# Attention followed by a token-mixing MLP: a mask built later, two scalings and one cast on other engines, token mixing three matmuls on

## The chip, the cores and the metric

The kernel runs on one core of a Trainium2 chip. The metric is the device time in microseconds (us) of one launch. Five engines work side by side: TensorE (PE in the profile), VectorE (DVE), ScalarE (ACT), GpSimd (POOL) and SyncE (SP), which here only issues DMAs. GpSimd and ScalarE issue DMAs too. Each engine takes its instructions in the order of its own list, and waits on semaphores for the others.

## The reference

There are 8 batches of 576 tokens, 8 heads of 64. First comes attention with a band of 32 positions to either side and 8 global tokens, which see all and are seen by all; then a residual MLP with a mixing over tokens and one over channels.

```python
scores = scale * np.matmul(q, k.transpose(0, 1, 3, 2))
mask = (np.abs(pos[:, None] - pos[None, :]) <= 32) | is_global[:, None] | is_global[None, :]
attn = softmax(np.where(mask, scores, -1e9))
x = (attn @ v) with the heads side by side            # (8, 576, 512)
tok = np.einsum('ts,bsd->btd', w_tok, alpha1 * x + beta1)
u = x + lam * tok
ch = np.maximum((alpha2 * u + beta2) @ w_ch1, 0.0) @ w_ch2
out = u + lam * ch
```

Inputs and output are fp32; the matmuls are fed in bf16 and fp16.

## The kernel before

**Stages.** The tokens of all batches make 36 tiles of 128 tokens. The channel MLP takes them in 9 groups of 4 tiles (GROUPS, L34): group 0 is batch 0 without its last 64 tokens, group 1 is batch 1 likewise, and a tile ("S", p) holds the last 64 tokens of two batches. A group is 128 steps, called slots here, each with one matmul of 512 columns: slots 0 to 63 compute W1 times the transposed tiles UT into HT (L559 to L567), slots 64 to 127 HT times W2 (L569). While group g runs, the attention and the token mixing of batch g + 1 are woven between its matmuls: `weave` (L84) spreads a list of small functions over a stretch of slots, and `timed` (L1070) does so for loads, transposes and copies. So the order on every engine follows from the slot numbers; there is no other planner. Within one slot the woven functions come before what `timed` put there, and these before the matmul.

**The opening.** Batch 0 has nothing to hide behind. Its order is written by hand: FIRST (L45) is a list of short names, looked up in `ops` (L922) and run from left to right; a name with ":n" uses PSUM bank n, and "sp:n" issues n spare matmuls whose result nobody reads. The names that matter here:
- `ck0..3`, `cq0..3`: casts of K and Q of two heads at a time to bf16 (L618, L622). CK names the engine of each K cast: A is ScalarE, D VectorE, P GpSimd.
- `tk`, `tq`: transposes on TensorE (L633); `kt`, `qv`: their copies out of PSUM (L637, L649).
- `gx` (L257) masks the gathered rows of the global tokens; `gt` (L693) transposes them into bank 1; `ge0` copies global K (L703) and half of global Q (L708) out of it, `ge1` the other half of global Q (L708), `gte` both once more for later (L697).
- `ct` casts the last 64 tokens of K and Q (L927), `tt` transposes them.
- `GM` (L852) builds the mask of the global keys, three instructions on VectorE: a comparison of positions with the global positions into a scratch tile, then two halves of the mask. `G` (L272) multiplies it with the exponentials `eg0`, `eg1` of the global scores in EG.
- `s20` and the like are scores (L351), `e...` their exponentials (L360), `pg`, `pt` masked probabilities (L317, L326), `q` and `pvx`, `pvy` the products with V.
- `va`, `vb` copy V to Vo, shifted by 64 rows.

**Batch 1.** Its attention is woven over slots 12 to 88 of group 0 (`first_attention`, L1038), the row sums of w_tok and the copies of wt4o at slot 89 (`late_rows`, L1031), its token mixing over slots 98 to 112. Each head pair ends with `norm_x`, `norm_y` on VectorE (L427) and `scale_x`, `scale_y`, which multiply by alpha1 * lam into XL (L445, L462, L463). `xl_eng` (L429) chooses the engine of the last two. A token tile (L509) is five matmuls, then `finish_u`:

```python
        nc.vector.tensor_tensor(out=x, in0=ps, in1=x, op=ALU.add)
        ...
        nc.gpsimd.tensor_tensor(out=ub, in0=x, in1=A2, op=ALU.mult)
        nc.sync.dma_start_transpose(out=UT[g % 2][:, :, js], in_=ub)
```

The first matmul of group 1 reads all four transposed tiles in UT.

**Batch 2 in group 0.** Its K, Q and V are loaded by GpSimd from slot 1 on, its K and Q are transposed by DMA from SyncE's queue over slots 44 to 75 (`xbars`, L1060), V is copied to Vo by two DMAs from SyncE's queue (`copy_vo`, L223), the gathered global rows are transposed at slots 98 and 100 (L266), and `qpad` (L234) copies QT to QP on VectorE at slots 101, 105, 109 and 113.

Of the kernel before, what the change touches and what calls it, by code (L numbers as in the profile page):

```python
# [10 lines left out]
FP16 = mybir.dt.float16  # L11
# [3 lines left out]
ALU = mybir.AluOpType  # L15

P = 128
S = 576
# [24 lines left out]
    [(7, 1), (7, 2), ("S", 3), (7, 3)],  # L43
]
FIRST = """  # L45
kgz vez io ktz pgz gb1 gbm:0 W0 gbc ar0 pz1 ar1 gath ck0 ar2 pgc tk0:1 sp:3 cq0 mask idn tq0:2 sp:16 V0 pz3 GM
qv0 V1 pz2 cq1 V2 tq1:3 kt0 cq2 V3 tq2:4 sp:1 ck2 qv1 qv2 ck1 tk2:5 V4 kt2 ck3 tk1:6 wki cq3 gat1 kt1 tk3:0 wi
kt3 gx tq3:2 ct qv3 gt:1 tt:3 sp:3 ge0 gte fz ktt ge1 qtt z20:4 s20:5 gk1:6 e201 la e200 z21:0 z11:2 s11:1
gk0:3 b1t eg1 va1 s21:5 e111 z00:4 s00:6 eg0 z10:1 sp:2 va2 e210 s10:3 vb1 G e211 z01:0 sp:2 e001 s01:5 e100
lb:6 e011 pz0 e010 pg2 z31:1 s31:5 lc v1f qz0 qz1 u0 pt2 ab:0 abe sp:2 e310 q2:6 e000 wt1:1 ra2 wt3:4 sp:2 we1  # L50
pg0 rd2 pvx2:6 e101 vb2 pt0 e311 pvy2:1 e110 q0:3 nx2 we3 wt0:5 pg1 ra0 wt2:2 nr2 ny2 we0 wt4:6 xl2 rd0 we2
q1:4 pt1 z30:1 s30:5 pvx0:3 we4 xm2 pvy0:2 nx0 ra1 rs:6 e300 beta rd1 e301 nr0 pg3 pvy1:1 re pvx1:3 ny0 pt3
xl0 q3:4 tm2:5 ra3 nr1 ny1 kc0 kc1 rd3 xm0 u1 nx1 pvy3:6 pvx3:2 ad2 xl1 tm0:4 nx3 xm1 u2 u3 u4 nr3 ad0 ny3 qc0
qc1 tx2:3 tm1:5 xl3 xm3 tx0:4 ad1 bm0 tm3:6 ut0 ut2 tx1:5 ad3 ut1 bm1 bm2 tx3:4 gc1 ut3 kc2 kc3 b1i qc2 qc3
bm3 W1s bme
"""
PLACE = {t: (g, j) for g, ts in enumerate(GROUPS) for j, t in enumerate(ts)}

# [41 lines left out]
def kernel(ctx, tc, q, k, v, global_idx, alpha1, beta1, w_tok, alpha2, beta2, w_ch1, w_ch2, lam, out):  # L100
    nc = tc.nc
# [8 lines left out]
    def T(name, shape, dt):  # L110
        return cp.tile(list(shape), dt, name=name)
# [19 lines left out]
    C16 = T("C16", [P, S], FP16)  # L131
    C32 = T("C32", c32n.shape, FP32)
# [17 lines left out]
    EG = T("EG", [P, S], FP16)  # L150
    G = T("G", [P, 2, 704], FP16)
    GM = T("GM", [P, 2, S], FP16)
# [8 lines left out]
    HTt = T("HT", [P, 16 * DM], BF16)  # L161
# [5 lines left out]
    mask = T("mask", [P, NW, 64], FP16)  # L167
# [16 lines left out]
    gbc = T("gbc", [P, 8], FP32)  # L184
    gsel = T("gsel", [P, 8], FP32)
    gval = T("gval", [P, 1], FP32)
# [17 lines left out]
    QST = XR[:, 8:12, :].rearrange("p a b -> p (a b)").rearrange("p (h j d) -> p h j d", h=H, j=4)  # L204
    TST = SR[:, 1, :]
    WTB = HTt[0:96, 0 : 6 * S].rearrange("p (c s) -> p c s", c=6)

    def xs(t):
        return SR[:, t[1] % 2, :] if t[0] == "S" else XR[:, 4 * (t[0] % 3) + t[1], :]
# [13 lines left out]
    def copy_vo(b):  # L223
        ve, vo = Ve[b % 2], Vo[b % 2]
        nc.sync.dma_start(out=vo[0:64], in_=ve[64:128, 0:4])
        nc.sync.dma_start(out=vo[64:128], in_=ve[0:64, 1:5])
# [141 lines left out]
    def sc_unit(b, hp, u):  # L368
        def f():
            ps = sc_ps()  # L370
            sc_mm(ps, b, hp, u)
            sc_exp(ps, b, hp, u)
            if u == 2:
                probs_q(b, hp)
                probs_k(b, hp)

        return (0.6, f)
# [14 lines left out]
    def gq_pv(b, hp):  # L392
        def f():
            ps = pv_ps()
            gq_mm(ps, b, hp)
            gq_hi(ps, hp)
            gq_lo(ps, hp)

        return (0.9, f)
# [27 lines left out]
        nc.vector.tensor_tensor(out=xo, in0=pv[:, :, :, 0:64], in1=rb, op=ALU.mult)  # L427

    def xl_eng(b, hp):  # L429
        return nc.vector if (b, hp) in ((0, 3),) else nc.gpsimd  # L430

    def pv_tiles(ps, b, hp, i0, i1):
        for i in range(i0, i1):
# [49 lines left out]
    def pv_y(b, hp):  # L483
        st = {}

        def f3():
            st["ps"] = pv_ps()
            pv_mms(b, hp, 3, st["ps"][:, 0:130])

        def f4():  # L490
            pv_mms(b, hp, 4, st["ps"][:, 130:260])
            norm_y(st["ps"], b, hp)
            scale_y(b, hp)

        return [(0.75, f3), (0.4, f4)]
# [13 lines left out]
    def tok_tile(b, i):  # L509
        par = b % 2  # L510

        def f():
            ps = pv_ps()
            cs = slice(128 * i, 128 * i + 128)
            for s in range(4):
                mm(ps, wtT[:, s, cs], XL[par][:, s, :], s == 0, False)
            mm(ps, wtT[:, 4, cs] if par == 0 else wt4o[:, cs], XL4[par], False, True)
            finish_u((b, i), ps)

        return (1.1, f)  # L520

    def tok_shared(p):
        def f():
            ps = pv_ps()
            for s in range(5):
                for par in range(2):
                    l = wt4o[:, 512:S] if s == 4 and par == 1 else wtT[:, s, 512:S]
                    mm(ps[64 * par : 64 * par + 64, :], l, XL4[par] if s == 4 else XL[par][:, s, :], s == 0, s == 4)
            finish_u(("S", p), ps)

        return [(1.1, f)]

    def gap(w):
        return (w, lambda: None)
# [11 lines left out]
    def token_mix(b):  # L546
        a = [tok_tile(b, i) for i in range(4)]
        if b % 2 == 1:
            a += tok_shared(b // 2)
        return a  # L550
# [103 lines left out]
    def tr_pair(b, hp):  # L654
        def f():
            psq, psk = pv_ps(), pv_ps()
            pair_tr(psq, QB0[b], hp)
            pair_tr(psk, KB0, hp)
            pair_k(psk, b, hp)
            for a in range(2):  # L660
                pair_q(psq, hp, a)

        return (0.6, f)
# [111 lines left out]
    def ld_wt():  # L775
        g_.dma_start(out=WTB, in_=w_tok.rearrange("(j p) s -> p j s", j=6))

# [72 lines left out]
        nc.vector.tensor_tensor(out=mask, in0=bd, in1=m9, op=ALU.mult)  # L850

    def gm():  # L852
        nc.vector.tensor_scalar(out=EG, in0=C16, scalar1=gval[:, 0:1], scalar2=None, op0=ALU.is_equal)
        for a in range(2):
            nc.vector.tensor_scalar(  # L855
                out=GM[:, a, :], in0=EG, scalar1=C32[:, 32 + a : 33 + a], scalar2=C32[:, 34 + a : 35 + a], op0=ALU.mult, op1=ALU.max
            )

    def b0_beta(par, eng):
# [3 lines left out]
    def wtok_tr(ps, k):  # L863
        ps = ps.bitcast(BF16)
        n = 128 if k < 4 else 64
        for j in range(6):
            nc.tensor.transpose(out=ps[0:n, 96 * j : 96 * j + 96], in_=WTB[:, j, 128 * k : 128 * k + n], identity=identb[0:96, 0:96])

# [49 lines left out]
    mlp0 = mlp(0)  # L918
    hb = {}
    CPY = {"A": nc.scalar.copy, "D": nc.vector.tensor_copy, "P": nc.gpsimd.tensor_copy}  # L920
    CK, QV, KC, QC, NY, PZ = "AAAD", "ADDD", "AAAA", "AAPP", "AADA", "PAAA"
    ops = {  # L922
        "idn": lambda: nc.scalar.copy(out=ident, in_=identb),
        "kgz": kz_fill,
# [97 lines left out]
    for w in FIRST.split():  # L1022
        n, _, b = w.partition(":")
# [14 lines left out]
    def first_attention(b):  # L1038
        s = [[sc_unit(b, hp, u) for u in range(3)] for hp in range(HP)]
        t_ = [tr_pair(b, hp) for hp in range(HP)]  # L1040
        q_ = [gq_pv(b, hp) for hp in range(HP)]
        w = [pv_x(b, hp) + pv_y(b, hp) for hp in range(HP)]
        a = [t_[0], tr_tail(b), gap(1.2), t_[1], gap(0.8), s[0][0], t_[2], gap(0.3), s[0][1], s[0][2], t_[3], gap(0.3)]
        a += [s[1][0], s[1][1], s[1][2], gap(0.4)]
        a += [gk_all(b, pv_ps), gap(0.5), q_[0], gap(0.6), s[2][0], s[2][1]] + w[0] + [q_[1], s[2][2], s[3][0], s[3][1]] + w[1] + [q_[2], s[3][2], gap(0.9)]
        return a + w[2][0:3] + [q_[3]] + w[2][3:] + [gap(0.9)] + w[3]
# [30 lines left out]
    for g in range(9):  # L1077
        base = mlp(g) if g else mlp0
        slots = [[] for _ in range(129)]
        nb = g + 2  # L1080
        if nb < NB:
            if g == 0:
                timed(prefetch(nb) + prefetch_v(nb), slots, 1, 42)
            else:
                timed(prefetch(nb), slots, 1, 34)
            timed(xbars(nb), slots, 44, 75)
            slots[78 if g else 118].append(lambda: copy_vo(nb))
            if nb % 2 == 0:
                pr = nb // 2
                slots[1].insert(0, lambda pr=pr: gather(pr))  # L1090
                slots[44] += [lambda: gather_x(0), lambda: gather_x(1)]
                slots[84 if g else 98].append(lambda pr=pr: gather_tr(pr, 0))
                slots[87 if g else 100].append(lambda pr=pr: gather_tr(pr, 1))
            timed([lambda hp=hp: qpad(hp) for hp in range(HP)] + [lambda: gcols(nb)], slots, 89 if g else 101, 105 if g else 122)
            if nb + 1 < NB:
                timed(prefetch_v(nb + 1), slots, 85 if g else 122, 96 if g else 127)

        def wrap(i):
            def f():
                for s in slots[i]:  # L1100
                    s()
                base[i]()

            return f

        items = [wrap(i) for i in range(128)] + base[128:]
        if g == 0:
            for i in range(9):
                items[i] = lambda i=i: [s() for s in slots[i]]
        if g == 0:  # L1110
            parts = [(first_attention(1), 12, 88), ([(1.0, late_rows)], 89, 90), (token_mix(1), 98, 112)]
        elif g + 1 < NB:
            parts = [(attention(g + 1), 2, 83), (token_mix(g + 1), 97, 115 if g < 3 else 122)]
        else:
            parts = []
        weave(items, parts)
# [30 lines left out]
```

## Time and profile before

| | |
|---|---|
| median of 14 runs | 389.71 us |
| lowest and highest | 387.49 and 390.97 us |
| the profiled execution, its own time | 388.54 us |
| its span in the profile | 386.8 us |
| TensorE busy | 375.2 us |
| VectorE, GpSimd, ScalarE busy | 225.3, 210.4, 175.1 us |
| granted clock of TensorE, mean | 0.995 |
| moved by DMA | 47.87 MB, 124 GB/s |

A line of a timeline reads: start (us from the span's start), length, engine, line of the kernel, operation, output<-inputs, shape, how many in a row; in brackets the idle time of the engine just before, and what released it. "SPq" is SyncE issuing a DMA: the time is that of the issue, and the data move later. A line of the list of waits reads: who waited, for whom, total us, how often, longest. Where a mark of landing is named in the text, it is the time at which the trace shows the last of a DMA's completion signals.

### The profile page before, as it was taken

The page shows a single profiled execution, that of the slowest core. Times are in us where ns is not written, and L with a number is a line of the kernel's source. Part 1 is how long each engine was busy: PE and PEld are TensorE (multiplying, and loading weights), DVE is VectorE, ACT ScalarE, POOL GpSimd, SP SyncE. Part 2 cuts the span into 40 slices and gives each one's busy share as a digit, 9 for nine tenths or more (in the row PEclk, how much of TensorE's full clock was granted, in tenths as well). Part 3 has the DMA queues.
Part 4 walks back from the last instruction along what each step waited for, and adds up shares of the span by engine and source line. Part 5 has one row for each costly group of instructions (what it writes and reads, how often), then busy time and mean ns, then how long its engine had stood idle before and what let it go on. Part 6 is the DMA issues. An engine that isn't in the chain of part 4 may idle for free.

```text
span 386.8 us, 8196 instructions
## 1 busy us (share of the span) xinstructions
PE 375.2 (97%) x3120; PEld 208.7 (54%) x3120; DVE 225.3 (58%) x585; ACT 175.1 (45%) x349; POOL 210.4 (54%) x273
## 2 busy tenths in 40 slices
PE   6899999999999999999999999999999999999996
PEld 3469566445654665456545664466456654444443
DVE  7887566984477557945595559545864554014023
ACT  6687874017800881067305840386028700730720
POOL 7978729786668844894388647963241335000000
PEclk9899999999999999999999999999999999999999
DMA  7999999969989994999497999799240013101002
GB/s 238 168 224 271 190 206 143 176 98 183 153 149 147 156 152 95 119 152 151 108 127 127 155 141 101 130 150 146 84 91 20 3 56 81 42 19 63 29 27 81
DMA packets 160836, 47.87 MB, mean 124 GB/s; under 512 B 147537, under 2 KB 154521, under 8 KB 160798
## 3 DMA queue, kind: packets, MB, share of 16 engines
q0 software_dynamic: 98288, 17.05, 66.0%
q1 hardware_dynamic: 61678, 29.71, 37.9%
q10 hardware_dynamic: 832, 0.60, 0.5%
q8 instruction: 24, 0.39, 0.4%
q14 instruction: 14, 0.11, 0.1%
HBM read 38.90 MB, written 9.44 MB: 125 GB/s over the span
## 4 chain that ended last, share of the span: by engine, by line
PE 84%; DVE 5%; DMA 5%; POOL 2%; ACT 1%; issue 1%; SPq 1%; ACTq 0%; POOLq 0%; DVEq 0%
PE bank L127 83%; DMA Vo<-Ve 2%; DMA QT<-Qb 2%; DMA XR<-in_q_dram 1%; POOL XL L445 1%; DVE PT L331 1%; POOL XL L463 1%; PE bank L899 0%; DVE PGQ L324 0%; POOL XL L462 0%; DVE Kb L622 0%; DVE GM L855 0%; PE bank L633 0%; DVE W L649 0%; ACT HT L565 0%
## 5 line engine op out<-in xcount | busy, mean ns | idle before, releaser
L127 PE MATMUL bank<-UT,W 128*128 128x512 bf16 x576 | 159.3, 379 | 0.1
L127 PE MATMUL bank<-W,HT 128*128 128x512 bf16 (+2 forms) x592 | 139.9, 373 | 0.0
L565 ACT ACTIVATE HT<-bank,bias 128x512 bf16<-128x512 f32 x128 | 88.0, 687 | 53.1 <-PE bank L127 52.3
L366 ACT ACTIVATE E<-bank 128x416 f16<-128x416 f32 (+1 forms) x84 | 41.8, 514 | 114.8 <-PE bank L127 114.0
L127 PEld LDWEIGHTS <-HT 128*128 128x128 bf16 (+1 forms) x610 | 54.4, 98 | 53.7 <-issue 1.9
L445 POOL TENSOR_TENSOR XL<-XR,LA 128x384 bf16<-128x384 f32 x31 | 31.5, 1015 | 71.2 <-DVE XR L427 52.9
L127 PEld LDWEIGHTS <-W 128*128 128x128 bf16 (+1 forms) x658 | 51.5, 97 | 25.8 <-issue 0.5
L580 DVE TENSOR_TENSOR OT<-bank,LAM 128x512 f32<-128x512 f32 (+2 forms) x37 | 24.9, 674 | 53.9 <-PE bank L127 53.6
L506 POOL TENSOR_TENSOR UB<-XR,A 128x512 bf16<-128x512 f32 x28 | 35.8, 1290 | 20.0 <-DVE XR L501 16.7
L127 PE MATMUL bank<-RG,G 128*128 128x65 f16 x320 | 43.0, 193 | 0.5 <-DVE RG L388 0.4
L127 PE MATMUL bank<-XL,wtT 128*128 128x512 bf16 (+2 forms) x240 | 41.6, 326 | 0.0
L127 PE MATMUL bank<-Ve,PT 128*128 128x65 f16 x300 | 41.2, 194 | 0.0
L127 PEld LDWEIGHTS <-PT 128*128 128x128 f16 x540 | 30.9, 98 | 16.6
L127 PEld LDWEIGHTS <-G 128*128 128x128 f16 x320 | 30.7, 97 | 15.8 <-DVE RG L388 0.9
L221 POOL DMA_DIRECT2D Ve<-in_v_dram x40 | 34.2, 876 | 0.2
L127 PEld LDWEIGHTS <-KT 128*128 128x128 bf16 (+1 forms) x324 | 23.4, 100 | 19.9 <-issue 3.1
L127 PE MATMUL bank<-Vo,PT 128*128 128x65 f16 x240 | 33.3, 192 | 0.5 <-DMA Vo<-Ve 0.5
L214 POOL DMA_DIRECT2D Qb<-in_q_dram x30 | 26.7, 891 | 7.6 <-DMA W<-in_moe_w_ch_dram 4.5
L214 POOL DMA_DIRECT2D Kb<-in_k_dram x30 | 26.8, 894 | 4.1 <-DMA W<-in_moe_w_ch_dram 3.9
L127 PE MATMUL bank<-QP,KT 128*128 128x144 bf16 (+1 forms) x252 | 28.7, 223 | 0.1
L127 PEld LDWEIGHTS <-wtT 128*128 128x128 bf16 (+1 forms) x240 | 18.7, 99 | 17.8 <-issue 1.9
L427 DVE TENSOR_TENSOR XR<-bank,rd 128x384 f32<-128x384 f32 (+1 forms) x61 | 26.3, 431 | 2.1
(161 smaller groups left out, 411.6 us busy)
## 6 DMA issues: line engine op xcount, KB each, us to landing
out_dram<-XR SPq DMA_DIRECT2D x31, 256.0 KB
W<-in_moe_w_ch_dram POOLq DMA_DIRECT2D x4, 1024.0 KB, 16.8
Vo<-Ve SPq DMA_DIRECT2D x14, 260.0 KB
Ve<-in_v_dram POOLq DMA_DIRECT2D x24, 128.0 KB, 6.6
Kb<-in_k_dram POOLq DMA_DIRECT2D x24, 128.0 KB, 6.4
Qb<-in_q_dram POOLq DMA_DIRECT2D x24, 128.0 KB, 6.6
Ve<-in_v_dram POOLq DMA_DIRECT2D x16, 96.0 KB, 6.2
XR<-in_k_dram SPq DMA_DIRECT2D x2, 512.0 KB
```

The lines of the kernel that those rows point to most:

```text
L127: nc.tensor.matmul(out=o, lhsT=l, rhs=r, start=st, stop=sp, skip_group_check=True)
L214: nc.gpsimd.dma_start(out=dst[0:n, c, :].rearrange("p (h d) -> p h d", d=D), in_=src[b, :, c * P : c * P + n, :].rearrange("h p d -> p h d"))
L221: nc.gpsimd.dma_start(out=Ve[b % 2][r0 : r0 + hi - lo, c, :, 0:D], in_=v[b, :, lo:hi, :].rearrange("h p d -> p h d"))
L331: nc.vector.tensor_tensor(out=bass.AP(pt.tensor, pt.offset + 64 + 128 * par, [p0, [256, n], [1216, 2], [1, 64]]), in0=bass.AP(e.tensor, e. ...
L366: nc.scalar.activation(out=eb(b, hp)[:, UOFF[u] : UOFF[u + 1]], in_=ps[:, 0:n], func=AF.Exp, bias=0.0, scale=0.125)
L427: nc.vector.tensor_tensor(out=xo, in0=pv[:, :, :, 0:64], in1=rb, op=ALU.mult)
L445: xl_eng(b, hp).tensor_tensor(out=XL[b % 2][:, 0:3, cs], in0=XR[:, base : base + 3, cs], in1=lb, op=ALU.mult)
L463: e.tensor_tensor(out=XL4[par][r0 : r0 + 64, cs], in0=SR[r0 : r0 + 64, (b // 2) % 2, cs], in1=LA1[r0 : r0 + 64, cs], op=ALU.mult)
L506: nc.gpsimd.tensor_tensor(out=ub, in0=x, in1=A2, op=ALU.mult)
L565: nc.scalar.activation(out=HT[:, ec, :], in_=st[ec], func=AF.Relu, bias=b_, scale=1.0)
L580: nc.vector.tensor_tensor(out=ot, in0=ps, in1=LAM[:, lo:hi], op=ALU.mult)
```

## The change

- In FIRST, `GM` moves from ahead of `qv0` to behind `va1`; `G` moves from ahead of `e211` to behind `pg2`; `ck3` moves ahead of `tk2` and, by CK, from VectorE to ScalarE; `ge1` moves ahead of `gte`.
- The comparison in `GM` is written to IG, an unused part of HT, and no longer to EG.
- `scale_x` and `scale_y` of batch 1's head pairs 1 and 3 go from GpSimd to VectorE.
- Batch 1's token mixing is woven over slots 101 to 114 and no longer 98 to 112: its five tiles start at slots 101, 103, 106, 108 and 111 where they started at 98, 100, 103, 106 and 109.
- In group 0, `copy_vo` of batch 2 goes from slot 118 to 104.

```diff
--- before.py
+++ after.py
@@ -43,16 +43,16 @@
     [(7, 1), (7, 2), ("S", 3), (7, 3)],
 ]
 FIRST = """
-kgz vez io ktz pgz gb1 gbm:0 W0 gbc ar0 pz1 ar1 gath ck0 ar2 pgc tk0:1 sp:3 cq0 mask idn tq0:2 sp:16 V0 pz3 GM
-qv0 V1 pz2 cq1 V2 tq1:3 kt0 cq2 V3 tq2:4 sp:1 ck2 qv1 qv2 ck1 tk2:5 V4 kt2 ck3 tk1:6 wki cq3 gat1 kt1 tk3:0 wi
-kt3 gx tq3:2 ct qv3 gt:1 tt:3 sp:3 ge0 gte fz ktt ge1 qtt z20:4 s20:5 gk1:6 e201 la e200 z21:0 z11:2 s11:1
-gk0:3 b1t eg1 va1 s21:5 e111 z00:4 s00:6 eg0 z10:1 sp:2 va2 e210 s10:3 vb1 G e211 z01:0 sp:2 e001 s01:5 e100
-lb:6 e011 pz0 e010 pg2 z31:1 s31:5 lc v1f qz0 qz1 u0 pt2 ab:0 abe sp:2 e310 q2:6 e000 wt1:1 ra2 wt3:4 sp:2 we1
-pg0 rd2 pvx2:6 e101 vb2 pt0 e311 pvy2:1 e110 q0:3 nx2 we3 wt0:5 pg1 ra0 wt2:2 nr2 ny2 we0 wt4:6 xl2 rd0 we2
-q1:4 pt1 z30:1 s30:5 pvx0:3 we4 xm2 pvy0:2 nx0 ra1 rs:6 e300 beta rd1 e301 nr0 pg3 pvy1:1 re pvx1:3 ny0 pt3
-xl0 q3:4 tm2:5 ra3 nr1 ny1 kc0 kc1 rd3 xm0 u1 nx1 pvy3:6 pvx3:2 ad2 xl1 tm0:4 nx3 xm1 u2 u3 u4 nr3 ad0 ny3 qc0
-qc1 tx2:3 tm1:5 xl3 xm3 tx0:4 ad1 bm0 tm3:6 ut0 ut2 tx1:5 ad3 ut1 bm1 bm2 tx3:4 gc1 ut3 kc2 kc3 b1i qc2 qc3
-bm3 W1s bme
+kgz vez io ktz pgz gb1 gbm:0 W0 gbc ar0 pz1 ar1 gath ck0 ar2 pgc tk0:1 sp:3 cq0 mask idn tq0:2 sp:16 V0 pz3
+qv0 V1 pz2 cq1 V2 tq1:3 kt0 cq2 V3 tq2:4 sp:1 ck2 qv1 qv2 ck1 ck3 tk2:5 V4 kt2 tk1:6 wki cq3 gat1 kt1 tk3:0 wi
+kt3 gx tq3:2 ct qv3 gt:1 tt:3 sp:3 ge0 ge1 gte fz ktt qtt z20:4 s20:5 gk1:6 e201 la e200 z21:0 z11:2 s11:1
+gk0:3 b1t eg1 va1 GM s21:5 e111 z00:4 s00:6 eg0 z10:1 sp:2 va2 e210 s10:3 vb1 e211 z01:0 sp:2 e001 s01:5 e100
+lb:6 e011 pz0 e010 pg2 G z31:1 s31:5 lc v1f qz0 qz1 u0 pt2 ab:0 abe sp:2 e310 q2:6 e000 wt1:1 ra2 wt3:4 sp:2
+we1 pg0 rd2 pvx2:6 e101 vb2 pt0 e311 pvy2:1 e110 q0:3 nx2 we3 wt0:5 pg1 ra0 wt2:2 nr2 ny2 we0 wt4:6 xl2 rd0
+we2 q1:4 pt1 z30:1 s30:5 pvx0:3 we4 xm2 pvy0:2 nx0 ra1 rs:6 e300 beta rd1 e301 nr0 pg3 pvy1:1 re pvx1:3 ny0
+pt3 xl0 q3:4 tm2:5 ra3 nr1 ny1 kc0 kc1 rd3 xm0 u1 nx1 pvy3:6 pvx3:2 ad2 xl1 tm0:4 nx3 xm1 u2 u3 u4 nr3 ad0 ny3
+qc0 qc1 tx2:3 tm1:5 xl3 xm3 tx0:4 ad1 bm0 tm3:6 ut0 ut2 tx1:5 ad3 ut1 bm1 bm2 tx3:4 gc1 ut3 kc2 kc3 b1i qc2
+qc3 bm3 W1s bme
 """
 PLACE = {t: (g, j) for g, ts in enumerate(GROUPS) for j, t in enumerate(ts)}
 
@@ -205,6 +205,8 @@
     TST = SR[:, 1, :]
     WTB = HTt[0:96, 0 : 6 * S].rearrange("p (c s) -> p c s", c=6)
 
+    IG = HTt[:, 5888 : 5888 + S].bitcast(FP16)
+
     def xs(t):
         return SR[:, t[1] % 2, :] if t[0] == "S" else XR[:, 4 * (t[0] % 3) + t[1], :]
 
@@ -427,7 +429,7 @@
         nc.vector.tensor_tensor(out=xo, in0=pv[:, :, :, 0:64], in1=rb, op=ALU.mult)
 
     def xl_eng(b, hp):
-        return nc.vector if (b, hp) in ((0, 3),) else nc.gpsimd
+        return nc.vector if (b, hp) in ((0, 3), (1, 1), (1, 3)) else nc.gpsimd
 
     def pv_tiles(ps, b, hp, i0, i1):
         for i in range(i0, i1):
@@ -850,10 +852,10 @@
         nc.vector.tensor_tensor(out=mask, in0=bd, in1=m9, op=ALU.mult)
 
     def gm():
-        nc.vector.tensor_scalar(out=EG, in0=C16, scalar1=gval[:, 0:1], scalar2=None, op0=ALU.is_equal)
+        nc.vector.tensor_scalar(out=IG, in0=C16, scalar1=gval[:, 0:1], scalar2=None, op0=ALU.is_equal)
         for a in range(2):
             nc.vector.tensor_scalar(
-                out=GM[:, a, :], in0=EG, scalar1=C32[:, 32 + a : 33 + a], scalar2=C32[:, 34 + a : 35 + a], op0=ALU.mult, op1=ALU.max
+                out=GM[:, a, :], in0=IG, scalar1=C32[:, 32 + a : 33 + a], scalar2=C32[:, 34 + a : 35 + a], op0=ALU.mult, op1=ALU.max
             )
 
     def b0_beta(par, eng):
@@ -918,7 +920,7 @@
     mlp0 = mlp(0)
     hb = {}
     CPY = {"A": nc.scalar.copy, "D": nc.vector.tensor_copy, "P": nc.gpsimd.tensor_copy}
-    CK, QV, KC, QC, NY, PZ = "AAAD", "ADDD", "AAAA", "AAPP", "AADA", "PAAA"
+    CK, QV, KC, QC, NY, PZ = "AAAA", "ADDD", "AAAA", "AAPP", "AADA", "PAAA"
     ops = {
         "idn": lambda: nc.scalar.copy(out=ident, in_=identb),
         "kgz": kz_fill,
@@ -1084,7 +1086,7 @@
             else:
                 timed(prefetch(nb), slots, 1, 34)
             timed(xbars(nb), slots, 44, 75)
-            slots[78 if g else 118].append(lambda: copy_vo(nb))
+            slots[78 if g else 104].append(lambda: copy_vo(nb))
             if nb % 2 == 0:
                 pr = nb // 2
                 slots[1].insert(0, lambda pr=pr: gather(pr))
@@ -1108,7 +1110,7 @@
             for i in range(9):
                 items[i] = lambda i=i: [s() for s in slots[i]]
         if g == 0:
-            parts = [(first_attention(1), 12, 88), ([(1.0, late_rows)], 89, 90), (token_mix(1), 98, 112)]
+            parts = [(first_attention(1), 12, 88), ([(1.0, late_rows)], 89, 90), (token_mix(1), 101, 114)]
         elif g + 1 < NB:
             parts = [(attention(g + 1), 2, 83), (token_mix(g + 1), 97, 115 if g < 3 else 122)]
         else:
```

## The prediction on record

> **What bounds the kernel now.** I read the page's busy line first, then the list of what TensorE (PE) waited for, then the timelines of PE, VectorE (DVE), SyncE's queue (SP) and GpSimd (POOL) around each edit.
>
> ```profile
> PE 375.2 (97%) x3120; PEld 208.7 (54%) x3120; DVE 225.3 (58%) x585; ACT 175.1 (45%) x349; POOL 210.4 (54%) x273
> ```
>
> PE is the bound: of 386.8 us it is idle for 11.6. By the table of stretches 6.5 of these lie before 30 us, 3.5 after its last matmul, and some 1.6 between. These entries of its list of waits touch the edits (total, times, longest):
>
> ```profile
> PE bank L127 <- DMA Vo<-Ve: 0.5, 1, 0.5
> ...
> PE bank L127 <- POOL XL L463: 0.3, 1, 0.3
> PE bank L127 <- DVE W L708: 0.3, 1, 0.3
> ```
>
> The L708 wait is in the opening, at 14.80 us; the XL wait at 73.56, in batch 1's token mixing; the Vo wait at 93.44, in group 1. The work of PE is the same in both kernels, so the end moves by the waits that go minus the waits that come. The opening on DVE:
>
> ```profile
> 7.39 0.36 DVE L853 TENSOR_SCALAR EG<-C,gval 128x576 f16<-128x576 f16 x1
> 7.79 1.59 DVE L855 TENSOR_SCALAR GM<-EG,C 128x576 f16<-128x576 f16 x2
> 9.29 1.11 DVE L622 CAST Kb<-XR 128x512 bf16<-128x512 f32 x2
> ```
>
> The mask takes 7.39 to 9.29 and the next casts follow at once. The token mixing, on DVE and on SP (L501 adds a token tile, L506 on POOL scales it, L507 transposes it into UT):
>
> ```profile
> 75.16 0.28 DVE L269 CAST KGT<-bank 128x128 bf16<-128x128 f32 x1
> 75.60 0.69 DVE L501 TENSOR_TENSOR XR<-bank,XR 128x512 f32<-128x512 f32 x1 [0.16 <-PE bank L127]
> 76.21 0.28 DVE L269 CAST QGT<-bank 128x128 bf16<-128x128 f32 x1
> 76.88 0.91 DVE L237 COPY QP<-QT 64x576 bf16<-64x576 bf16 x2 [0.40 <-DMA QT<-Qb]
> 77.82 0.69 DVE L501 TENSOR_TENSOR XR<-bank,XR 128x512 f32<-128x512 f32 x1
> ```
>
> Two of the four adds are done before the first copy of QP, which waits for the transposes of Q to land. Then SP, and PE at the start of group 1:
>
> ```profile
> 76.67 7.86 SPq L507 DMA_TRANSPOSE UT<-UB  x5
> 84.63 0.51 SPq L586 DMA_DIRECT2D out_dram<-XR  x1
> 85.75 0.50 SPq L225 DMA_DIRECT2D Vo<-Ve  x1
> 86.36 0.53 SPq L226 DMA_DIRECT2D Vo<-Ve  x1
> ```
> ```profile
> 80.90 4.27 PE L127 MATMUL bank<-W,HT 128*128 128x512 bf16 x19
> 85.02 0.59 PE L127 MATMUL bank<-UT,W 128*128 128x512 bf16 x2
> ```
>
> Group 1's first matmul needs all four transposed tiles of batch 1. Nineteen matmuls of 0.2164 us from 80.90 end at 85.01: no wait at 85.02. But it is close: the trace's landing marks put the fourth tile at 84.39, 0.6 us ahead.
>
> **What the Trainium skill says.** "DMA: Bandwidth & Descriptors", section "Queues, rings and completion order": on each DMA engine the descriptors of one issuing queue are consumed in ring order. The trace agrees: the Vo copies issued at 85.75 move their first packet at 88.36, when the output store issued before them has moved its last (88.02). "PSUM — Partial Sum Buffer", section "PSUM bank collisions raise a hardware error": two engines on one bank and quadrant must be kept apart, reads from reads too. The trace agrees: L708 on DVE and L699 on ScalarE (ACT) both only read bank 1, and L708 stands 0.56 us for L699. "SBUF — State Buffer", section "Who interferes with whom": a DVE instruction with two SBUF inputs contends with a POOL instruction that reads SBUF. The trace agrees: the pair L331 takes 0.83 us at 22.77 with POOL idle and 1.35 at 25.61 beside POOL's L462.
>
> **The change part by part.**
>
> *Mask and casts in the opening.* 1.90 us leave DVE at 7.39 and K3's cast (0.35 to the next start) at 11.52; K3 costs ACT 0.6, inside its idle 0.99 before 11.23. But what follows is held by loads: by the landing marks Q's third part is there at 9.03 and the fourth at 11.22, the second gather at 11.64, the tail of Q at 12.89. The last gives the cast at 12.97, PE's transposes at 13.64, three spare matmuls and the first scores at 14.30, none of which the edit moves. What can go is PE's standing from 14.30 to 14.80, for the second glob_q, which no longer comes behind ACT's two copies: at most 0.47. The mask returns at about 16.3, 1.9 to 2.0 us on DVE ahead of the chain that starts with L324 at 21.78, into idle stretches of 0.39, 0.82 and 0.58 = 1.79; POOL's memsets beside it are the unknown. So at 21.78 the opening is between 0.45 earlier and 0.3 later; I take 0.3 earlier. G behind L324 costs nothing: its reader comes over 1 us later.
>
> *Scalings on DVE.* POOL loses two sets of about 1.00 + 0.46 + 0.45 = 3.8 us and is done at 68.75 instead of 73.51. DVE gains two sets of 0.55 + 0.28 + 0.28 (its row for batch 0) = 2.2. The first set stands before L388 at 63.26, whose idle 0.27 takes part of it; PE could be held 0.1, its neighbour RG. The second stands before the copies of wt4o and the beta row, but without POOL beside them these take about 0.3 + 0.3 + 0.67 instead of 0.50 + 1.03 + 0.83, and end near 72.9 instead of 73.19. They are needed at 73.95 in the new order. The loss at 73.56 (0.48 between where the matmul was due and where it started) goes.
>
> *Token mixing later, and the Vo copies from slot 118 to 104.* This is where I expect the price. With the tiles at slots 101, 103, 106, 108 and the QP copies at 101, 105, 109, the instruction order is now tile 0, QP copy, tile 1, QP copy, tiles 2 and 3: **tile 1 stands behind a QP copy that waits for QT**, where two tiles went ahead of it. And on SP the two Vo copies now stand **between the second and third transposes**. QT comes by DMA that nothing in the change makes earlier (landing mark 76.77): its loads waited in a backlog of GpSimd's DMA queue. Step by step: QP copy 76.88 to 77.79, tile 1's add to 78.51, POOL's scaling (1.24) to 79.8, transpose 1 issued 79.85 to 81.05, two Vo issues 1.2 to 1.7 to about 82.5, transposes 2 and 3 at 1.2 each to about 84.9. Tiles 2 and 3 have left POOL by 81.4 and 82.6, so SP is last. The fourth transpose was issued until 83.16 and landed 84.39, 1.23 later: 86.1 if the Vo data do not hold it. In ring order they do: Vo starts about 1.2 after its first issue, 82.4, and the five other pairs in the trace moved their data in 2.35 to 3.6 us; transposes need 0.65 each after that and 0.65 to the landing mark. That gives 86.8 to 88.0. Between 86.1 and 88.0 I take 86.9. In exchange Vo lands seven us ahead of its use and the 0.47 at 93.44 goes.
>
> *Sum against the profiled execution* (388.54; span 386.8, 1.74 around it): group 1 starts at 86.9 instead of 85.02, +1.9; Vo -0.47; **+1.4, or 389.9**. The 0.3 of the opening and the 0.48 of the scalings do not count: PE would be ready at 84.2 and wait for tiles whose time DMA sets. The median of the runs shown, 389.71, is 1.2 above the profiled execution; I add the sum to it: 391.1.
>
> **The rivals.**
> - *Tiles late, as above, 0.63* with both ends: 86.1 to 88.0 is +0.6 to +2.5, 390.3 to 392.2. A PE idle of over 2 us might also make the clock drop for a window; at 14.65 it stood at 0.50 for 3.4 us, which would cost 1.7 more: 392.8. Against that: the stretch from 7.8 to 11.2, about half filled by spare matmuls, was followed by full clock. I give it 0.05 of the 0.63.
> - *It evens out, 0.14*: QT lands about a us earlier in most runs, or the Vo data slip past the transposes. The point of balance is a fourth tile at 85.02 + 0.47 = 85.5. About 389.7.
> - *Faster, 0.23*: QT is there before DVE reaches the QP copy (75.35) and SP's Vo issues cost only their 1.1 us; then tile 1 is added by 77.0, and the fourth tile can land by 84.3 and hold nobody. All three waits are saved, 0.48 + 0.47 + 0.3 = 1.25: 388.5. It decides from 85.5 downwards. For it: the edits stand exactly at the waits that the list names. Against: the 0.40 that DVE already waits for QT.
> - That the order does not change as the diff says is excluded: the instruction lists of both kernels show it.
>
> **How the numbers follow.** About 0.2% (0.8 us) can be told from no change. The first case is slower by more than that, except for its lower edge: 0.63 slower, 0.14 within, 0.23 faster. The likeliest case alone spans 390.3 to 392.2. For 8 in 10 the range runs down to 388.4 (half of the faster case left out) and up to 392.3 (the clock's case left out).
>
> **What would show it.** Right: a PE wait of 1.5 to 2 us at the first UT matmul of group 1, released by the DMA into UT; DVE idle about 1.5 us before the first QP copy; no Vo wait in group 1; no XL wait. In the opening: no wait of PE for L708, mask near 16.3. Wrong: group 1 starting without a wait, or a new wait in the opening that DVE's mask ends.

## The result, and the profile after

The changed kernel takes **396.01 us** (median of 10 runs, 394.10 to 399.44), the kernel before beside it 389.76 (47 runs). The ratio is 1.0161, interval 1.0136 to 1.0186: slower by about 6.2 us. (A ratio leaves out executions over 1.5% above the fastest of their kernel, so it need not be the quotient of two medians.) The forecast of slower was right, its size (391.1, at most 392.3) was not.

The profiled execution of the changed kernel has a span of 395.3 us, 8.5 more than the one before; these two lie about 1 us on either side of their medians, which is why 8.5 here is 6.2 there. The line numbers of the changed kernel are 2 higher than before (L508 is the scaling on GpSimd, L509 the transpose). Its page, busy line and granted clock:

```profile
PE 376.5 (95%) x3120; PEld 209.1 (53%) x3120; DVE 226.5 (57%) x590; ACT 175.5 (44%) x350; POOL 206.5 (52%) x267
...
PEclk9899999996999999999999999999999999999999
```

PE's work is about the same, its share of the span is not: time was added in which it stands. The 6 in the clock row is new; it sits in the slice from 88.9 us on. The list of what PE waited for:

```profile
PE bank L127 <- DMA UT<-UB: 6.7, 1, 6.7
...
PE bank L127 <- DVE RG L390: 0.7, 3, 0.3
```

The Vo wait, the XL wait and the wait for the global-Q copy are gone. One wait of 6.7 us has come. PE where groups 0 and 1 meet (start, length):

```profile
82.23 3.84 PE L127 MATMUL bank<-W,HT 128*128 128x512 bf16 x17
92.81 1.01 PE L127 MATMUL bank<-UT,W 128*128 128x512 bf16 x2 [6.73 <-DMA UT<-UB]
93.61 0.55 PE L127 MATMUL bank<-QP,KT 128*128 128x144 bf16 x3
```

PE is ready at 86.1 and goes on at 92.81. Its first two matmuls then take 1.01 where the same two took 0.59 before. The table by stretches (span of each, then PE busy and, behind the engines, the clock) says why:

```profile
86.00:89.27 3.27, 0.07 (x1) 0.00 (x0) 2.43 (x7) 0.00 (x0) 3.27 (x5) 1.00 1.30 150
89.27:92.81 3.54, 0.00 (x1) 0.03 (x2) 0.00 (x0) 0.00 (x0) 3.54 (x5) 0.50 2.58 136
92.81:96.10 3.29, 3.29 (x13) 1.64 (x14) 0.00 (x0) 1.59 (x3) 2.77 (x4) 0.50 1.68 201
```

The clock fell to half 3.2 us after PE had stopped and stayed there until 96.10, so 3.29 us of group 1 were worked at half speed: about 1.6 us lost. Now the chain that feeds UT, first on DVE, then on POOL, then on SP:

```profile
76.04 0.68 DVE L503 TENSOR_TENSOR XR<-bank,XR 128x512 f32<-128x512 f32 x1
78.42 0.91 DVE L239 COPY QP<-QT 64x576 bf16<-64x576 bf16 x2 [1.71 <-DMA QT<-Qb]
79.36 0.69 DVE L503 TENSOR_TENSOR XR<-bank,XR 128x512 f32<-128x512 f32 x1
79.97 0.90 DVE L239 COPY QP<-QT 64x576 bf16<-64x576 bf16 x2
80.90 1.29 DVE L503 TENSOR_TENSOR XR<-bank,XR 128x512 f32<-128x512 f32 x2
```
```profile
80.13 1.27 POOL L508 TENSOR_TENSOR UB<-XR,A 128x512 bf16<-128x512 f32 x1 [2.02 <-DVE XR L503]
81.67 2.49 POOL L508 TENSOR_TENSOR UB<-XR,A 128x512 bf16<-128x512 f32 x2 [0.26 <-DVE XR L503]
84.12 1.27 POOL L508 TENSOR_TENSOR UB<-SR,A 128x512 bf16<-128x512 f32 x1
85.33 4.26 POOL L223 DMA_DIRECT2D Ve<-in_v_dram  x5
89.55 0.91 POOL L216 DMA_DIRECT2D Kb<-in_k_dram  x1
```
```profile
78.14 4.89 SPq L509 DMA_TRANSPOSE UT<-UB  x2
83.20 0.48 SPq L227 DMA_DIRECT2D Vo<-Ve  x1
83.78 0.53 SPq L228 DMA_DIRECT2D Vo<-Ve  x1
84.48 5.01 SPq L509 DMA_TRANSPOSE UT<-UB  x3
```

So far it is the order that the prediction named: one tile, the QP copy with its wait for QT (1.71 idle), the second tile behind it, Vo between the second and third transposes. The fourth transpose is issued at 86.55. But by the landing marks it is there at 92.67, and the row on POOL that the prediction had not looked at is the last but one: as soon as its last scaling is done, GpSimd goes on to the loads of batch 3's V, and then of its K and Q. The packets that the DMA engines began in each us, counted from the trace (tr: 256-byte packets of transposes; loads: 128-byte packets of GpSimd's queue):

```
us           84   85   86   87   88   89   90   91   92   93
changed  Vo  37   49   42    0    0    0    0    0    0    0
         tr   0    0  202  310   14  314  177   43  287  189
      loads   0    0    0  280  794  558  590  904  412  567
before   tr 404  108    0    0    0    0    0    0    0    0
      loads   4  772  209  633  828  279  208  303  322  708
```

A transpose has 512 of the 256-byte packets. Before, the four needed ones and most of the fifth had gone when the loads began at 85. In the changed kernel Vo's data take 84 to 87, the third transpose just gets through, and the fourth spreads from 88.5 to 91.1 among some 1,600 packets of loads. My theory from here: Vo alone moves the transposes by about the 2 us foreseen, and **this pushes them into the loads of the next batch**, which is the rest.

### The profile page after: what moved, and what is told of

Same layout as the page of the kernel before. It is cut to its first block, busy times and chain, and to the rows that moved or that the text cites. A ratio compares the mean times of both kernels' runs of the same rounds, so it can differ in the third digit from the quotient of the medians.

```text
span 395.3 us, 8191 instructions
## 1 busy us (share of the span) xinstructions
PE 376.5 (95%) x3120; PEld 209.1 (53%) x3120; DVE 226.5 (57%) x590; ACT 175.5 (44%) x350; POOL 206.5 (52%) x267
## 4 chain that ended last, share of the span: by engine, by line
PE 83%; DMA 6%; DVE 6%; POOL 3%; issue 1%; ACT 1%; SPq 1%; POOLq 0%; DVEq 0%
PE bank L127 82%; DMA HT<-in_moe_w_tok_dram 3%; DMA UT<-UB 2%; DMA QT<-Qb 1%; POOL Ve L223 1%; POOL UB L508 1%; DVE XR L429 1%; POOL KQG L255 1%; PE bank L901 0%; ACT HT L567 0%; DVE XR L583 0%; DVE RG L390 0%; DVE OT L582 0%; DVE XR L503 0%; DVE QP L645 0%
## 5 line engine op out<-in xcount | busy, mean ns | idle before, releaser
L447 POOL TENSOR_TENSOR XL<-XR,LA 128x384 bf16<-128x384 f32 x29 | 29.0, 1001 | 79.3 <-DVE XR L429 51.4
L508 POOL TENSOR_TENSOR UB<-XR,A 128x512 bf16<-128x512 f32 x28 | 35.8, 1289 | 25.7 <-DVE XR L503 22.4
L326 DVE TENSOR_TENSOR PGQ<-E,gqm 128x80 f16<-128x80 f16 x60 | 9.3, 196 | 36.5 <-ACT E L368 36.4
L583 DVE TENSOR_TENSOR XR<-OT,XR 128x512 f32<-128x512 f32 (+2 forms) x33 | 27.5, 832 | 1.6
```

What stands on the lines that cost most here:

```text
L326: nc.vector.tensor_tensor(out=pg[:, :, c0 : c0 + 16].rearrange("p c (a g) -> p c a g", a=2), in0=gq_in, in1=gq_m, op=ALU.mult)
L447: xl_eng(b, hp).tensor_tensor(out=XL[b % 2][:, 0:3, cs], in0=XR[:, base : base + 3, cs], in1=lb, op=ALU.mult)
L583: nc.vector.tensor_tensor(out=x, in0=ot, in1=x, op=ALU.add)
```

## The experiments

Every ratio is against the kernel before on the same chip, in 5 rounds; the medians of before were 389.85 to 390.38.

**1. Vo back at slot 118, the rest of the change kept.**

```diff
-            slots[78 if g else 104].append(lambda: copy_vo(nb))
+            slots[78 if g else 118].append(lambda: copy_vo(nb))
```


> The changed kernel with the Vo copies of batch 2 back at slot 118; mask, cast, scalings and the later token mixing stay. Theory A (the loss is in the Vo copies between the transposes: their data go first, and the third and fourth transposes then move beside the loads of batch 3's V): the fourth tile lands near 86.1, group 1 starts within 0.5 us of 85.9, the clock stays full, and the time falls by 5.5 to 6.5 to 389.3 to 390.5. Rival B (tile 1 behind the QP copy does it alone): the wait stays above 4 us and the time above 394. Rival C (the opening or the scalings cost several us): no change by more than 2 us.

Measured 391.48, ratio 1.0029 (1.0005 to 1.0054). Of the 6.2 us some 5 are gone, and with them the wait for UT; that rules out B and C as main causes. It missed the range that I gave, since another wait has grown:

```profile
PE bank L127 <- DMA Vo<-Ve: 2.8, 1, 2.8
```

It was 0.5 in the kernel before. All of SP's work stands about 2.5 us later than there (the Vo copies are issued at 88.17, in the kernel before at 85.75), so Vo, at the end, now moves among the loads. Whoever comes last meets them.

**2. Token mixing back at 98 to 112, Vo kept at 104.**

```diff
-(token_mix(1), 101, 114)
+(token_mix(1), 98, 112)
```


> The changed kernel with batch 1's token mixing back at slots 98 to 112; the Vo copies stay at 104, so that they now stand ahead of the fourth transpose alone. Theory A: three transposes are issued about 2 us earlier, the fourth still moves behind Vo's data but is done before batch 3's V loads fill the engines: group 1 waits 0.3 to 1.5 us, no clock drop, time 389.5 to 391.0. Rival B (tile 1 behind the QP copy): no wait at all, 389 to 389.7. Rival D (ring order behind Vo's data alone makes the loss, the V loads have no part): a wait of over 3 us stays, over 392.5.

Measured 393.43, ratio 1.0064 (1.0036 to 1.0091); the profile shows a wait for UT of 2.6 us and half clock for 3.4 us. Worse than theory A expected; the time lies in D's range, the wait below D's 3 us, so that this run decides nothing between the two. With one transpose behind Vo instead of two, there is still a price, so the later mixing is not needed for a loss, but it more than doubles it.

**3. The loads of batch 3's V moved into group 1.**

```diff
+            if g == 1:
+                timed(prefetch_v(nb), slots, 36, 43)
...
-                timed(prefetch_v(nb + 1), slots, 85 if g else 122, 96 if g else 127)
+                if g:
+                    timed(prefetch_v(nb + 1), slots, 85, 96)
```


> The changed kernel with only the five loads of batch 3's V taken out of group 0's slots 122 to 126 and put in group 1's slots 36 to 42. Theory A: Vo's data still go first, but the transposes behind them take 0.7 us each: the fourth lands at 87 to 88, group 1 waits 1 to 2 us instead of 6.7, the clock does not drop, time 390.3 to 391.7 (what was predicted for the change itself). Rival D (ring order behind Vo alone): the fourth tile still lands after 91, 395 to 396.5.

Measured 395.43, ratio 1.0144 (1.0117 to 1.0171), a wait of 5.5 us. By the letter of the expectation this speaks for D. POOL shows that it tested nothing:

```profile
81.69 1.27 POOL L508 TENSOR_TENSOR UB<-SR,A 128x512 bf16<-128x512 f32 x1
82.90 0.93 POOL L216 DMA_DIRECT2D Kb<-in_k_dram  x1
83.83 0.89 POOL L216 DMA_DIRECT2D Qb<-in_q_dram  x1
```

A slot number only orders a queue. With V out of the way GpSimd goes straight to the K and Q loads, with the same 128-byte packets, at the same place.

**4. Spare matmuls through the wait.**

```diff
...
+        if g == 0:
+            last = items[127]
+            items[127] = lambda: (last(), spare(60, 3))
```


> The changed kernel with 60 spare matmuls of 256 columns (0.11 us each at full clock, 6.5 in all, results read by nobody) behind group 0's last matmul, so that the array works through the wait at group 1. Theory A with the clock as a second term: the tiles still land at 92.7, but the first matmuls of group 1 run at full clock and not at half for 3.3 us: 1.3 to 1.8 us faster than the changed kernel, 394.2 to 394.7. Rival E (the clock costs nothing here): 395.8 to 396.2.

Measured 394.51, ratio 1.0116 (1.0084 to 1.0149): 1.5 us less than the changed kernel by the medians (the two intervals overlap a little), and the clock stays full.

```profile
85.52 6.71 PE L127 MATMUL bank<-C 128*128 128x256 bf16 x60
92.06 0.38 PE L127 MATMUL bank<-UT,W 128*128 128x512 bf16 x1
```

Sixty useless matmuls in front of group 1 made the changed kernel faster. Group 1 takes 39.6 us from its first matmul to group 2's, against 41.2 in the changed kernel. The clock is thus a second term of 1.5 us; the wait itself is the first.

**5. No loads for batch 3.** The kernel leaves out batch 3's K, Q and V, so that its outputs are computed from old buffers.

```diff
-            else:
+            elif g > 1:
                 timed(prefetch(nb), slots, 1, 34)
...
-            if nb + 1 < NB:
+            if nb + 1 < NB and g:
                 timed(prefetch_v(nb + 1), ...
```


> The changed kernel without the loads of batch 3's V, K and Q (left out: batch 3 is computed from what the buffers hold), so that GpSimd's DMA queue is quiet while the transposes behind Vo move. The run with V moved to group 1 did not test this, since GpSimd went on at once to the K and Q loads, with the same 128-byte packets. Theory A (those packets stretch the transposes): the fourth tile lands about 88, group 1 waits 2 to 2.7 us instead of 6.7 and the clock drops for one window at most: 391 to 393. Rival D (only the place behind Vo counts): wait over 4.5 us, 394.5 to 396.

Measured 391.33, ratio 1.0032 (1.0010 to 1.0053), within theory A's range and outside D's. PE where the groups meet:

```profile
83.73 2.32 PE L127 MATMUL bank<-W,HT 128*128 128x512 bf16 x10
88.12 0.59 PE L127 MATMUL bank<-UT,W 128*128 128x512 bf16 x2 [2.07 <-DMA UT<-UB]
88.55 0.34 PE L127 MATMUL bank<-QP,KT 128*128 128x144 bf16 x3
...
89.12 1.41 PE L127 MATMUL bank<-UT,W 128*128 128x512 bf16 x3
```

SP's order is that of the changed kernel, with the fourth transpose issued at 85.66 (86.55 there); it landed at 87.98 instead of 92.67. The packets:

```
us           84   85   86   87   88
no loads Vo  43   52    0    0    0
         tr   0  145  467  412  401
      loads   0    0    0    0    0
```

Here is the place behind Vo without the loads: a wait of 2.07 us. That it comes so near to the 1.9 of the prediction is partly luck: the tile lands 1.1 us after the likeliest 86.9, and PE is ready 1.0 after 85.02. Not all of the other 4.7 is the loads: from issue to landing the fourth transpose takes 2.32 us here and 6.12 in the changed kernel, 3.8 more, and the remaining 0.9 is that it was issued that much earlier here, as the third was too, before the loads of batch 3 would have begun. Whether the loads cost this by their packets or by GpSimd's issuing was not separated; the packet counts speak for the packets. The last line of the profile shows the clock: three matmuls in 1.41 where 0.81 is usual. A wait of 2.07 was enough to halve it, from 89.19 to 92.61.

**6. Vo at slot 110**, behind the four transposes that group 1 needs and ahead of the fifth, which it does not.

```diff
-            slots[78 if g else 104].append(lambda: copy_vo(nb))
+            slots[78 if g else 110].append(lambda: copy_vo(nb))
```


> The changed kernel with the Vo copies at slot 110 instead of 104: still ahead of the last transposed tile (the shared one), which group 1 does not need, but behind all four that it does. Theory A (the price is the place between the transposes): the fourth tile lands at 86 to 87, the wait at group 1 is under 1 us, and since Vo is issued about 1.7 us earlier than at slot 118 the Vo wait of 2.8 us that came with slot 118 shrinks below 1.5: 389.3 to 390.7. Rival B (later token mixing alone): group 1 still waits over 3 us, over 393.

Measured 388.93, ratio 0.9981 (0.9963 to 0.9999): slightly faster than the kernel before, 7 us faster than the changed one, by one number, and below the range of theory A. SP:

```profile
77.32 5.79 SPq L509 DMA_TRANSPOSE UT<-UB  x4
83.31 0.48 SPq L227 DMA_DIRECT2D Vo<-Ve  x1
83.90 0.53 SPq L228 DMA_DIRECT2D Vo<-Ve  x1
84.97 2.32 SPq L509 DMA_TRANSPOSE UT<-UB  x1
```

The profile has no wait for UT here and none for Vo. The loads have not gone away: the fifth transpose now meets them and lands at 92.72, and nobody waits for it then.

**7. Only the opening and the scalings (both_back), and the opening alone (open_only).** The first is the changed kernel with the edits of 1 and 2 together; the second also has `xl_eng` as before.

> The changed kernel with the Vo copies back at 118 and the token mixing back at 98 to 112, so that only the opening's edits and the two scalings are left of the change. If these cost nothing (theory A): 389.3 to 390.3, no wait for UT and a Vo wait under 1 us. If they bring the 0.5 of the XL wait: 389.0 to 389.6. If the opening is the hidden loss (rival C): over 391.

> The kernel before with the opening's edits alone (mask later in its own scratch, third K cast on ScalarE, order of the global copies). Theory A: 389.6 to 390.5, since the first scores wait for loads; rival C: over 391, if the mask in its new place or the K cast holds PE.

Measured 389.79, ratio 1.0000 (0.9980 to 1.0020), and 391.33, ratio 1.0030 (1.0012 to 1.0048). The first says that opening and scalings together are worth nothing that can be seen. The second is harder: by the letter it speaks for rival C, yet it should not be slower than the first, which has the same opening. Its profile shows a Vo wait of 2.0 us, where the first has 0.8, and half clock from 15.3 to 28.9 in the opening, and over its runs the mean granted clock was 0.989, against 0.995 for the kernel before and 0.997 for both_back. A clock 0.006 lower over 390 us is 2.5 us of work, more than the difference. Whether the new opening makes such drops or the longer Vo wait likelier, or they came by chance in these runs, stays open.

**8. The QP copies later (slots 107 to 119).**

```diff
-slots, 89 if g else 101, 105 if g else 122)
+slots, 89 if g else 107, 105 if g else 124)
```


> The changed kernel with the four QP copies at slots 107 to 119 instead of 101 to 117, so that three token tiles go ahead of the first of them on VectorE; Vo stays between the second and third transposes. Theory A (three things have to meet: a second tile held by the QP copy, Vo between the transposes, and the loads of batch 3): the second transpose goes 1.5 to 2 us earlier, Vo's data are done by 85.5 and the fourth tile lands at 86 to 88, before the loads are thick: wait of 0 to 1.5 us, 389 to 391.5. Rival F (the place behind Vo is enough, whatever the second tile does): over 394.

Measured 393.46, ratio 1.0103 (1.0064 to 1.0141). Three tiles now go ahead of the first copy of QP, and the wait for UT is 3.7 us in place of 6.7. Between the two expectations: holding the second tile is a part of the loss, about 2.3 us by the ratios (the intervals overlap a little), not a condition for it. Its fourth transpose is issued at 83.99, and lands at 88.47, still among the loads: 970 of their packets began while its own did, from 85.5 to 87.4.

**9. Vo ahead of all transposes (slot 92).**

```diff
-            slots[78 if g else 104].append(lambda: copy_vo(nb))
+            slots[78 if g else 92].append(lambda: copy_vo(nb))
```


> The changed kernel with the Vo copies at slot 92, ahead of all transposes and of one output store. Theory A: their data are away by 80, nothing stands before the transposes when they are issued, the fourth lands at 86 to 86.8, the UT wait is under 1 us and there is no Vo wait: 388.6 to 390. Rival F (Vo ahead of the transposes costs wherever it stands, since the ring is in order): the fourth tile is late by Vo's 2.4 to 3.6 us of data, 391 to 393.

Measured 390.65, ratio 1.0022 (1.0001 to 1.0043). The profiled execution has a span of 385.5, the shortest of all the profiles, with no wait for UT or Vo, as theory A said; but the runs' mean clock was 0.990, and the median is worse than A's range. Undecided as a version; against F the profile is clear.

**10. Which of the other edits the version of 6 needs.** First with the old opening, then with the scalings on GpSimd:

```diff
-        return nc.vector if (b, hp) in ((0, 3), (1, 1), (1, 3)) else nc.gpsimd
+        return nc.vector if (b, hp) in ((0, 3),) else nc.gpsimd
```


> The version with Vo at slot 110 that ran at 388.9 beside 389.85, now with the opening of the kernel before (mask early in VectorE's list, third K cast on VectorE). If the opening's edits are worth nothing (theory A): the same, 388.6 to 389.3. If they cost (the opening alone ran 1.2 us over the kernel before): 387.5 to 388.2. If they help: 389.3 to 390.

> The version with Vo at slot 110, now with batch 1's scalings of head pairs 1 and 3 back on GpSimd. The wait for XL, 0.48 us in the kernel before, would come back unless the later token mixing already covers it: three matmuls of 0.216 us are 0.65 us, more than 0.48, so I expect no XL wait and 388.6 to 389.4. If the scalings are what saves: 389.4 to 390.

Measured 0.9975 (0.9953 to 0.9997) and 0.9961 (0.9941 to 0.9982), the latter at a median of 388.32: the best version, about 1.5 us faster than the kernel before. Neither the opening nor the scalings show a gain in it. The list of waits of the second has no XL wait: three matmuls more before the mixing already hide it, as expected. It does have two for UT, 1.7 us together, in an execution 2.6 us above its median.

**11. One edit at a time on the kernel before**: Vo at slot 107 alone, behind the four transposes with the old mixing; then Vo at 110 with the later mixing.

> The kernel before with one number changed: the Vo copies at slot 107, behind the four transposes that group 1 needs and ahead of the shared one; token mixing, scalings and opening as before. Theory A (Vo's place against the transposes and the loads is all): no UT wait, the Vo wait of 0.5 us goes, the XL wait stays: 0.3 to 0.7 us faster than the kernel before. If the later mixing is needed for the gain: no difference within 0.2.

> The kernel before with the token mixing at 101 to 114 and Vo at 110, opening and scalings as before. Theory A: 0.5 to 1.3 us faster than the kernel before, as the three versions with Vo at 110 (ratios 0.9961 to 0.9981); no XL wait, because the mixing now comes 0.65 us later. If opening or scalings carried the gain: no difference within 0.2.

Measured 389.12, ratio 0.9972 (0.9953 to 0.9991), and 388.82, ratio 0.9963 (0.9940 to 0.9986). Vo's place alone gains about 1.1 us, more than the 0.3 to 0.7 expected, though the interval reaches down to 0.4. The profile of the first has no wait for UT or Vo, only the two for XL (0.6 and 0.2); that of the second waits 1.2 for UT. What the later mixing adds can't be told from nothing.

## Why the prediction was wrong

**What held.** The place (group 1's first matmul, released by the transposes into UT), the order on DVE and SP that leads there, DVE's idle time before the first QP copy (1.71 against about 1.5), no Vo wait, no XL wait. The rivals that it evens out or gets faster are excluded. The ring order that the prediction took from the Trainium skill ("DMA: Bandwidth & Descriptors", "Queues, rings and completion order") held too, as far as the trace shows it: the third transpose began its packets at 86.41, when the last of Vo's were starting (86.85), and the fourth came behind it.

**The term that was mis-sized: "transposes need 0.65 each after that and 0.65 to the landing mark. That gives 86.8 to 88.0."** The fourth landed at 92.67. Its packets took 2.56 us (88.52 to 91.08) and the landing mark another 1.6. Experiment 5 splits the miss: without the loads of batch 3 the fourth lands at 87.98, inside what was stated; with them it takes 3.8 longer from issue to landing. The other 0.9 stood on the chain before that (QT, below). The working took its 0.65 from transposes that had the DMA engines to themselves, and never asked what else would move at 87. The section of the skill just named says, besides the order within a queue, that a DMA engine takes turns between the queues for which it has work, a packet at a time; I used the one sentence and not the other. The trace agrees in that both move together: 314 packets of transposes and 558 of loads began in the us from 89. The trace of before held the warning: there the fifth transpose, issued last, landed at 86.90, 3.6 us after its issue began at 83.33, and the Vo data began at 88.36 and landed only at 93.40, both beside those same loads. I priced Vo from the other pairs (2.35 to 3.6; there are six, not five) and left this one out.

**The clock, given 0.05.** It took half speed for 3.29 us of group 1, and experiment 4 gives 1.5 us back. The skill ("TensorE: Matmul & The Clock Gate", "Why this matters for your kernels") warns of idle gaps over about 3 us, which is laxer than these runs. I argued that a stretch half filled by spare matmuls had been followed by full clock; but here PE is empty, and even the 2.07 of experiment 5, close to the wait that I held for likeliest, halved the clock for 3.4 us. The likeliest case thus should have carried much of the 1.7 itself.

**The size of QT's lateness.** QT came at 78.4 and not at 76.8, so that the second transpose was issued at 81.43, not 79.85. Relative to PE, itself ready at 86.1 and not at 85.02, about 0.5 of this counts. In experiment 5 the second was issued at 79.72, as stated, but its issue took 2.4 where 1.2 was said; so the fourth came at the upper end of what was stated.

**Opening and scalings.** The wait for the global-Q copy did go, and the mask came at 17.00 (16.3 was said) and took 1.5 instead of 1.9. Yet the first scores started at 15.45, not at 14.30 or earlier, since the tail of Q, a load, came later (13.51, not 12.89). Group 0's W1 starts between 38.0 and 42.1 over all the profiles, with either opening, so that the 0.3 was too small to be seen; experiment 7 gives zero within 0.8 us. The scalings took POOL's load off, and the XL wait went; but DVE's extra work shows as a wait of PE for RG (L390) between 60 and 75 us, 0.3 to 1.1 us in all eleven profiles with these scalings on DVE and none in the other five, where I allowed 0.1; and experiment 10 finds no gain.

**The sum.** Between the two profiled executions, 8.5: the wait of 6.7, where 1.9 was said; 1.6 less speed; PE 0.9 later at the end of group 0, inside what the openings scatter; less about 0.8 for Vo and small gaps in group 1. From group 2 on both take 261.3 us.

## What to carry to other kernels

When a transfer is moved ahead of others, ask not only what it delays on its own queue, but what the delayed ones will then meet: price them beside the traffic that starts next, from a row of the trace in which the same thing already happened. Of a group of transfers let those go first that the bound engine needs first; here one number (slot 110 for 104) was 7 us. And to move a load in a program is not to move it in time: an idle queue takes the next one at once.

## What the runs showed of the hardware

How dear the sharing is: a transpose of 512 packets of 256 bytes, through in some 0.7 us when alone, took 1.8 to 2.6 us beside GpSimd's 128-byte packets (2.56, from 88.52 to 91.08, in the changed kernel), and Vo's 4,160-byte packets, 0.16 to 0.54 us each in experiment 5, took up to 0.99 in the kernel before.

A PE that stood for 2.1 to 6.7 us where the groups meet was followed by one or two stretches of 3.41 us at half clock in experiments 2, 3, 5 and 8 and the changed kernel. The 2.8 of experiment 1, the 2.0 of the opening alone and the 1.2 in the second version of experiment 11 were not. So gaps well under 3 us can cost it too, and the same gap need not. The clock records of these traces suggest why: their full stretches last 3.41 us or a multiple of it (6.83, 71.68), and what seems to count is how much of the wait falls into one such stretch. In the five that dropped, 2.0 to 3.4 us of it did; the 2.8 was cut in two by a border (1.4 and 1.4), the 2.0 as well (1.7 and 0.3). This is read from the traces afterwards: no run moved a wait against the borders, and in the opening less idle time in a stretch (1.3 to 1.9 us) was at times followed by half clock too.
